# Moving six matmuls of the output layer in front of the fourth product into the C bank

## The chip, the cores and the metric

The kernel runs on one core of a Trainium2 chip. The metric is the device time of one execution in microseconds. The engines have their own instruction queues, each served in order: TensorE (PE, with its weight loads shown as PEld), VectorE (DVE), ScalarE (ACT), GpSimd (POOL) and SyncE (SP), which here only issues DMAs. They wait for one another by semaphores.

## The reference

Two layers in a row, in float32. First an attention over channels, for each of 4 batches of 6080 tokens with 256 channels:

```
qn, kn = q, k divided by their norms over the tokens
a      = softmax(kn^T @ qn / tau)          # 256 x 256 for each batch
x      = v @ a                             # 6080 x 256
h      = max(x @ w_in, 0)                  # 2048 wide
out    = (h * h) @ w_out                   # 256 wide again
```

The kernel multiplies `a` into `w_in` once for each batch, so that the two products left are `v @ (a w_in)` and `h*h @ w_out`.

## The kernel before

**Precision.** A float32 operand is split into a high part and a low part, each rounded to the type that TensorE takes. One product is then three matmuls: high by high, low weights by high, high weights by low. A split takes a cast on ACT (the high part) and a subtraction on DVE (the low part).

**Groups.** After two blocks of tokens that are done in a plain way, the work goes in 184 groups, k = 0 to 183. A group is one block of tokens (512, in the last two blocks of a batch 480) and a quarter of the 2048 hidden channels. Products of both layers are done in the manner of Strassen and Winograd: on halves of the block and halves of the weights, seven block products instead of eight, with sums and differences formed by DVE.

**First layer, three banks of PSUM.** `product` (line 992) issues six matmuls: two parts of the hidden channels by three terms. Group k makes seven such products: `first_B` and `second_B` into a B bank, `first_H` and `second_H` into an H bank, and for the C bank `copy_C` (line 1199: ACT copies B's first product into C), `second_C`, `third_C` and `fourth_C` (line 1217). Between them the C bank is read: `copy_of_C` (ACT, after the second product), `add_C` (DVE, line 1241, after the third product: adds C to a block of x and applies the rectifier), `relu_C` (ACT, line 1235, after the fourth). As the fourth product writes into the bank that `add_C` reads, `fourth_C` waits for `add_C` of the same group. It also issues the loads of the later weight forms of group k + 2.

**Second layer, one group and two groups behind.** The rectified blocks of x are squared on ACT (`square_three`, three of them at once, and `square_last`), and combined on DVE: `two_sums`, `third_sum`, `last_sum`. They are split in three lots: "A" (`hi_A` on ACT, `lo_A` on DVE, lines 1158 and 1163), "S1" (`hi_S`, `lo_S`) and "S2". The products with W_out are windows of six matmuls each: `window_A1`, `window_A2`, `window_A3` use lot A of group k - 1; four `window_S` use lots S1 and S2 of group k - 2. `window_A2` multiplies the block a2 by the weight sum S4 and adds into a part of its own of the output bank. In six groups (`PLAIN`, line 1025) a window has three matmuls and the rest is done without sums.

**The order.** `PERIOD` (line 1279) lists the steps of one period by hand, each with its lag: 0 for the newest group, 1 and 2 for the groups behind. The steps of a period are issued in this order; each engine's queue keeps it. A text in place of a step ("act", "dve", "sq", "pe", "norms", "mid") is a point at which the attention of the next batch, running beside, puts in its own pieces: chunks of q and k with their Gram products, or products of `a` with w_in. At "pe" TensorE gets most of these pieces; "pe" stands between `second_H` and `window_A1`.

In the last period the three A windows are held back and issued later, by a loop of their own.

Of the kernel before, what the change touches and what calls it, by code (L numbers as in the profile page):

```python
# [32 lines left out]
def kernel(  # L33
# [1138 lines left out]
    def lo_S(k, which):  # L1172
        hi, lo = PA[k, which]
        vector.tensor_sub(lo, XG[k][:, :, SLOTS[which], :], hi.bitcast(F32))
# [75 lines left out]
    def next_v(k, j, do, i):  # L1250
        b, n, at_j = groups[k]
        at = order.index((b, n)) + 1
        if at_j == j and at < len(order):
            do(at, i)
# [21 lines left out]
    def lo_S2(k):  # L1276
# [37 lines left out]
        (1, third_sum),  # L1314
        (0, square_three),
        (1, window_A1),
        (1, lambda k: next_v(k, 2, lo_of_v, 1)),
        (1, last_sum),
        (0, fourth_C),
# [1 line left out]
        (None, late_step),  # L1321
        (0, first_sum_of_v),
        (1, lambda k: lo_S(k, "S1")),
        (1, window_A2),
        (0, relu_C),
        (1, lambda k: next_v(k, 1, lo_of_v, 0)),
        (1, window_A3),
# [260 lines left out]
```

## Time and profile before

| | |
|---|---|
| Median of 3 runs | 2068.84 us (2067.64 to 2071.0) |
| The profiled execution's own time | 2066.14 us |
| Its span, first to last instruction | 2064.3 us |
| PE, PEld busy | 2057.3 us, 2014.0 us |
| DVE, ACT busy | 1894.4 us, 1869.1 us |
| POOL busy | 350.6 us |
| Granted TensorE clock | 1.000 |

The profile is of one execution. Matmuls are pipelined: a matmul row lasts 0.28 us, but the next one begins 0.11 us later, so the pace of TensorE is read from starts, not from durations. The whole stretch of the 184 groups lies between about 157 and 2051 us of the span.

### The profile page before, as it was taken

What the parts mean: (1) busy time and instruction counts of PE and PEld (TensorE: products, weight loads), DVE (VectorE), ACT (ScalarE), POOL (GpSimd) and SP (SyncE); (2) the same over time, 40 slices, a digit from 0 to 9 for tenths busy, and PEclk for the clock granted to TensorE, in tenths of its full rate; (3) what the DMA queues carried; (4) which work ended last, traced back from release to release, by engine and by line L of the source; (5) the groups of instructions that cost most, each with busy time, mean ns of one, the idle gap of its engine ahead of it and who ended that gap; (6) DMA issues with size and microseconds to landing.
All of it is one profiled execution on the core that took longest, in us unless ns stands there. A gap on an engine that the chain in (4) does not pass through costs nothing.

```text
span 2064.3 us, 43463 instructions
## 1 busy us (share of the span) xinstructions
PE 2057.3 (100%) x17158; PEld 2014.0 (98%) x17158; DVE 1894.4 (92%) x2195; ACT 1869.1 (91%) x2379; POOL 350.6 (17%) x430
## 2 busy tenths in 40 slices
PE   9999999999999999999999999999999999999999
PEld 8789999999999999999999999999999999999999
DVE  7898999989999999989999999998999888888887
ACT  5888999989999999989989999989988988988987
POOL 0000111211222111211112111211121121121121
PEclk9999999999999999999999999999999999999999
DMA  9777888889999888889999988888999788787785
GB/s 362 226 223 277 262 254 268 244 263 313 306 282 303 287 260 259 246 258 295 292 302 266 335 260 263 252 262 251 294 286 308 235 243 253 236 248 247 237 241 153
DMA packets 258012, 549.78 MB, mean 266 GB/s; under 512 B 26672, under 2 KB 113072, under 8 KB 257808
## 3 DMA queue, kind: packets, MB, share of 16 engines
q1 hardware_dynamic: 201456, 469.02, 66.9%
q0 software_dynamic: 56352, 77.98, 18.8%
q8 instruction: 135, 2.21, 0.4%
q14 instruction: 69, 0.57, 0.1%
HBM read 433.59 MB, written 58.72 MB: 238 GB/s over the span
## 4 chain that ended last, share of the span: by engine, by line
PE 94%; DVE 2%; ACT 2%; DMA 1%; issue 0%; SPq 0%; DVEq 0%; ACTq 0%
PE ps_o L29 42%; PE ps_c L29 18%; PE ps_h L29 13%; PE ps_b L29 11%; PE gram L29 7%; PE ps_w L29 2%; DVE x L29 1%; ACT x L29 1%; DMA acc_w<-wi_kept 0%; DVE s_lo L29 0%; DMA v<-in_vT 0%; DVE A_lo L29 0%; ACT A_hi L29 0%; DMA wf<-wf_kept 0%; PE ps_end L29 0%
## 5 line engine op out<-in xcount | busy, mean ns | idle before, releaser
L29 DVE TENSOR_TENSOR x<-x 128x1024 f32<-128x1024 f32 (+2 forms) x549 | 465.0, 847 | 11.1
L29 PE MATMUL ps_c<-v_hi,wf 128*128 128x256 f32 (+1 forms) x2208 | 473.1, 279 | 1.8 <-DVE x L29 0.9
L29 POOL DMA_DIRECT2D o<-o x225 | 232.7, 1188 | 1344.0 <-ACT o L29 838.2
L29 DVE TENSOR_TENSOR s_lo<-x,s_hi 128x1024 fp32r<-128x1024 f32 (+1 forms) x366 | 441.3, 1207 | 13.5 <-ACT s_hi L29 13.2
L29 ACT CAST s_hi<-x 128x1024 fp32r<-128x1024 f32 (+1 forms) x366 | 382.7, 1046 | 72.8 <-DVE x L29 71.4
L29 ACT ACTIVATE x<-x 128x1536 f32<-128x1536 f32 (+4 forms) x384 | 405.4, 1056 | 34.6 <-DVE x L29 33.2
L29 DVE TENSOR_TENSOR A_lo<-x,A_hi 128x1536 fp32r<-128x1536 f32 (+2 forms) x183 | 313.3, 1712 | 76.3 <-ACT A_hi L29 73.3
L29 PEld LDWEIGHTS ps_c<-v_hi,wf 128*128 128x128 f32 x2208 | 374.0, 188 | 9.1 <-DVE x L29 5.9
L29 PE MATMUL ps_b<-v_hi,wf 128*128 128x256 f32 (+1 forms) x1472 | 309.9, 276 | 0.0
L29 PE MATMUL ps_h<-v_hi,wf 128*128 128x256 f32 (+1 forms) x1472 | 309.9, 276 | 0.0
L29 PE MATMUL ps_c<-v_lo,wf 128*128 128x256 f32 (+1 forms) x1104 | 304.9, 276 | 0.0
L29 ACT CAST A_hi<-x 128x1536 fp32r<-128x1536 f32 (+2 forms) x183 | 264.9, 1448 | 0.0
L29 PEld LDWEIGHTS ps_b<-v_hi,wf 128*128 128x128 f32 x1472 | 249.2, 188 | 0.1
L29 PEld LDWEIGHTS ps_h<-v_hi,wf 128*128 128x128 f32 x1472 | 249.2, 188 | 0.0
L29 PEld LDWEIGHTS ps_c<-v_lo,wf 128*128 128x128 f32 x1104 | 207.6, 188 | 0.1
L29 PE MATMUL ps_b<-v_lo,wf 128*128 128x256 f32 (+1 forms) x736 | 203.1, 276 | 0.0
L29 PE MATMUL ps_h<-v_lo,wf 128*128 128x256 f32 (+1 forms) x736 | 203.1, 276 | 0.0
L29 PE MATMUL ps_o<-A_hi,wo_hi 128*128 128x256 f32 (+1 forms) x897 | 191.2, 277 | 0.0
L29 PE MATMUL ps_o<-A_lo,wo_hi 128*128 128x256 f32 (+1 forms) x897 | 190.0, 276 | 0.0
L29 PE MATMUL ps_o<-A_hi,wo_lo 128*128 128x256 f32 (+1 forms) x897 | 189.9, 276 | 0.0
L29 PE MATMUL ps_o<-s_lo,wS_hi 128*128 128x256 f32 (+1 forms) x549 | 151.6, 276 | 0.3 <-DVE s_lo L29 0.2
L29 PE MATMUL ps_o<-s_hi,wS_hi 128*128 128x256 f32 (+1 forms) x549 | 151.6, 276 | 0.0
(172 smaller groups left out, 5132.2 us busy)
## 6 DMA issues: line engine op xcount, KB each, us to landing
wf<-wf_kept SPq DMA_DIRECT2D x368, 512.0 KB, 5.2
wf<-wf_kept SPq DMA_DIRECT2D x368, 384.0 KB, 5.3
o<-o POOLq DMA_DIRECT2D x114, 256.0 KB, 5.5
qk<-in_k SPq DMA_DIRECT2D x88, 256.0 KB, 5.2
qk<-in_q SPq DMA_DIRECT2D x88, 256.0 KB, 5.4
v<-in_vT SPq DMA_DIRECT2D x76, 256.0 KB, 4.9
out_T<-o POOLq DMA_DIRECT2D x152, 128.0 KB, 4.7
wf_kept<-wS SPq DMA_DIRECT2D x64, 256.0 KB, 5.7
```

Source lines behind the costliest of these rows:

```text
L29: return lambda *args, **kwargs: self.tc.keep_in_program_order(issue(*args, **kwargs))
```

## The change

One entry of the list `PERIOD` moves. `window_A2`, six matmuls for group k - 1, was issued after `fourth_C`, the point "norms" and two DVE steps; it is now issued directly after `window_A1`, ahead of `fourth_C`. No instruction is added or removed, and the steps of the other engines keep their order.

```diff
         (0, square_three),
         (1, window_A1),
+        (1, window_A2),
         (1, lambda k: next_v(k, 2, lo_of_v, 1)),
         (1, last_sum),
         (0, fourth_C),
         (None, "norms"),
         (None, late_step),
         (0, first_sum_of_v),
         (1, lambda k: lo_S(k, "S1")),
-        (1, window_A2),
         (0, relu_C),
         (1, lambda k: next_v(k, 1, lo_of_v, 0)),
         (1, window_A3),
```

So TensorE's order around the change was `third_C`, `second_H`, pieces at "pe", `window_A1`, `fourth_C`, pieces at "norms", `window_A2`, `window_A3`, `first_B` of the next group, and becomes `third_C`, `second_H`, pieces at "pe", `window_A1`, `window_A2`, `fourth_C`, pieces at "norms", `window_A3`, `first_B`.

## Rows read from the trace of the kernel before

**Rows 1.** The page: busy time by engine, and the chain that ended last.

```profile
PE 2057.3 (100%) x17158; PEld 2014.0 (98%) x17158; DVE 1894.4 (92%) x2195; ACT 1869.1 (91%) x2379; POOL 350.6 (17%) x430
...
PE 94%; DVE 2%; ACT 2%; DMA 1%; issue 0%; SPq 0%; DVEq 0%; ACTq 0%
```

**Rows 2.** Waits, whole span, weight loads: us in total, times, longest us.

```profile
PEld ps_c L29 <- DVE x L29: 5.9, 23, 0.4
```

**Rows 3.** Timeline of PE, group 141 (start us, us, instruction), and the next second_C.

```profile
1643.43 0.39 PE L29 MATMUL ps_o<-A_lo,wo_hi 128*128 128x256 f32 x2
1643.69 0.38 PE L29 MATMUL ps_c<-v_hi,wf 128*128 128x256 f32 x1
1643.91 0.28 PE L29 MATMUL ps_c<-v_lo,wf 128*128 128x256 f32 x1
...
1644.36 0.28 PE L29 MATMUL ps_c<-v_hi,wf 128*128 128x256 f32 x1
...
1648.55 0.28 PE L29 MATMUL ps_c<-v_hi,wf 128*128 128x256 f32 x1
```

**Rows 4.** Timeline of ACT, groups 141 to 142; idle time before and its releaser in brackets.

```profile
1644.32 1.49 ACT L29 ACTIVATE x<-x 128x1536 f32<-128x1536 f32 x1 [0.20 <-DVE x L29]
1645.72 0.58 ACT L29 ACTIVATE x<-ps_c 128x512 f32<-128x512 f32 x1
...
1647.66 0.59 ACT L29 COPY ps_c<-ps_b 128x512 f32<-128x512 f32 x1
1648.18 1.48 ACT L29 CAST A_hi<-x 128x1536 fp32r<-128x1536 f32 x1
...
1654.00 1.49 ACT L29 ACTIVATE x<-x 128x1536 f32<-128x1536 f32 x1 [0.20 <-DVE x L29]
```

**Rows 5.** Timeline of DVE, the same stretch.

```profile
1642.95 0.68 DVE L29 CUSTOM_DVE_ANT_0 x<-x,ps_c 128x512 f32<-128x512 f32 x1
...
1649.69 1.76 DVE L29 TENSOR_TENSOR A_lo<-x,A_hi 128x1536 fp32r<-128x1536 f32 x1 [1.20 <-ACT A_hi L29]
...
1652.63 0.68 DVE L29 CUSTOM_DVE_ANT_0 x<-x,ps_c 128x512 f32<-128x512 f32 x1
```

**Rows 6.** All waits of ACT and DVE in 1614.6 to 1973.9 us (groups 139 to 175).

```profile
ACT s_hi L29 <- DVE x L29: 29.9, 29, 1.6
ACT x L29 <- DVE x L29: 7.6, 37, 0.2
...
DVE A_lo L29 <- ACT A_hi L29: 36.7, 37, 1.2
DVE s_lo L29 <- ACT s_hi L29: 2.2, 9, 0.3
```

**Rows 7.** Two stretches: length, busy us and count of PE, PEld, DVE, ACT, POOL; clock, DMA.

```profile
610.00:840.00 230.00, 230.00 (x2031) 230.00 (x2030) 223.62 (x235) 221.64 (x275) 45.42 (x56) 1.00 0.91 275
1614.60:1973.90 359.30, 359.18 (x3111) 355.71 (x3109) 318.21 (x343) 321.66 (x408) 70.93 (x87) 1.00 0.82 244
```

**Rows 8.** Timeline of ACT and DVE, groups 71 to 72.

```profile
921.88 0.60 ACT L29 ACTIVATE x<-ps_c 128x512 f32<-128x512 f32 x1 [0.47 <-PE ps_c L29]
...
926.68 0.59 ACT L29 COPY x<-ps_c 128x512 f32<-128x512 f32 x1 [0.80 <-PE ps_c L29]
...
929.46 0.69 DVE L29 CUSTOM_DVE_ANT_0 x<-x,ps_c 128x512 f32<-128x512 f32 x1 [0.53 <-PE ps_c L29]
```

**Rows 9.** Timeline: fourth_C's last matmul and relu_C of group 43; copy_C, second_C of 70.

```profile
621.22 0.28 PE L29 MATMUL ps_c<-v_hi,wf 128*128 128x256 f32 x1
...
621.53 0.60 ACT L29 ACTIVATE x<-ps_c 128x512 f32<-128x512 f32 x1
...
903.03 0.59 ACT L29 COPY ps_c<-ps_b 128x512 f32<-128x512 f32 x1
...
903.92 0.28 PE L29 MATMUL ps_c<-v_hi,wf 128*128 128x256 f32 x1
```

**Rows 10.** The page's DMA issues: the later weight forms, KB each, us to landing.

```profile
wf<-wf_kept SPq DMA_DIRECT2D x368, 512.0 KB, 5.2
```

## The prediction

> **What bounds the kernel now.** I began with the busy times. TensorE is busy for the whole span and carries 94% of the chain that ended last, with VectorE and ScalarE at 92% and 91% [rows 1]. Read alone, this says that only TensorE's lost time matters. So I looked next for what TensorE waits for: one wait stands out, weight loads into the C bank behind VectorE, 5.9 us in 23 times [rows 2]. The timeline shows whose it is. In group 141 the last window of A ends its starts at 1643.43 + 0.11, and the first matmul of `fourth_C` starts at 1643.69, just behind `add_C`, which ended at 1642.95 + 0.68 = 1643.63 [rows 3, 5]. The reader should see a second loss here: the next matmul starts 0.22 us later (1643.91) and not the usual 0.11, so a wait, however short, costs about 0.11 more. I counted 63 groups whose `fourth_C` begins like this, with a first matmul of 0.38 us as in rows 3; the first starts at 170.53, the last at 1983.60 us, and 37 of them are all the groups from 139 to 175. Together they cost 5.9 + 63 x 0.11 = 12.8 us. That is all that the change aims at.
>
> The last question is who sets the pace where the waits stand, and this is what decides the forecast. In the stretch of those 37 groups, list what ScalarE and VectorE wait for: each other, and nothing else; no row names TensorE [rows 6]. Follow one turn by starts: the square of three blocks at 1644.32, `relu_C` at 1645.72 (1.40), `copy_C` at 1647.66 (1.94, with two more steps of ScalarE in it), `hi_A` at 1648.18 (0.52) [rows 4], `lo_A` at 1649.69 (1.51, it waits for `hi_A`), `add_C` at 1652.63 (2.94, with the two sums) [rows 5], and the next square of three at 1654.00 (1.37) [rows 4]. The sum is 9.68 us, and the 37 groups took 359.30 / 37 = 9.71 each [rows 7]. TensorE alone would need less: in 610 to 840 us it starts 2031 matmuls in 230.00 us without losing any, 0.1132 us each [rows 7], and a group of seven products and seven windows has 84, so 9.51 us. In this stretch the two slower engines turn in a loop of their own, TensorE is 0.20 us a group faster, and its wait in front of `fourth_C` is only the place where it is held back to their pace. Elsewhere, as in 610 to 840 us, it loses nothing and there is nothing to win.
>
> **The change part by part.** No instruction is added or removed; 184 windows of six matmuls (three where the group behind is one of the six plain ones) move ahead of six others. Three things follow.
>
> *The wait for `add_C`.* `fourth_C` now comes 6 x 0.113 = 0.68 us later (0.34 behind plain groups). In group 141 it would come 0.6 us after `add_C`, with no wait. TensorE then runs ahead until something else holds it. Next is `second_C`, which needs `copy_C`: 1648.55 against 1647.66 + 0.59 = 1648.25, a slack of 0.30 us [rows 3, 4]. So TensorE wins the one wait (0.15) and this slack once, and from then on stands in front of `second_C` for the same 0.20 us a group. The gain of the whole stretch is at most 0.15 + 0.30 = 0.45 us, kept at its end when TensorE becomes the slower one again, and not 37 x 0.2 = 7.4 us. If delay from ahead comes into the loop, the gain falls, to 0 or below.
>
> *`relu_C` waits longer.* It needs the end of `fourth_C`, which moves back by 0.68 us. In group 141 that costs nothing: `fourth_C` ends at 1644.36 + 0.28 = 1644.64 and `relu_C` starts at 1645.72, 1.08 later [rows 3, 4]. But in 30 groups, which lie in 16 separate runs between 206.0 and 1549.2 us, `relu_C` starts within 0.15 us of the end of `fourth_C`, as in group 43: 621.22 + 0.28 = 621.50 against 621.53 [rows 9]. They are the groups in which the other batch's pieces make TensorE long. There ScalarE gets the full 0.68, and behind `relu_C` are queued the cast of lot S2, the last square, `copy_C` and `hi_A`. What hides it: in most of these runs ScalarE waits again a little later. After group 71 it stood 0.80 us in front of the copy out of C after `second_C`, a product that does not move, and VectorE stood 0.53 us in front of the next `add_C` [rows 8]. So ScalarE takes up all of the 0.68 and VectorE all but 0.15. Cost about 0 for 13 of the runs, where I take group 71 as typical; 0.38 each if the cover is gone (below).
>
> It is gone in the stretches with Gram products, where ScalarE is busy 221.64 and VectorE 223.62 of 230.00 us [rows 7]. The delay of groups 43 and 44 travels with them until the loop meets TensorE again near group 70, where `second_C` starts at 903.92 and `copy_C` ends at 903.03 + 0.59 = 903.62, a slack of 0.30 [rows 9]. TensorE loses 0.68 - 0.30 = 0.38 us. This happens twice (batches 1 to 2, 2 to 3), and a first time behind a plain group with 0.34 - 0.30 = 0.04: together +0.80.
>
> *Short waits that do vanish.* In the shorter runs (groups 29, 73, 77, 81, 121, 125) one wait of `fourth_C` stands between two stretches that TensorE paces. These go, at up to 0.11 each: 0 to -0.7, I take -0.4, since the delay of 0.15 above eats some.
>
> *What is queued with the moved steps.* `window_A2` needs lot A, as `window_A1` just before it does, and writes into a bank that is open already: no new wait. `fourth_C` issues the loads of the later forms of group k + 2 on SP, so these go out 0.68 us later, in the same order on that queue. They land in 5.2 us [rows 10] and are wanted more than one turn (9.68) after the next `second_C`, 1648.55 + 9.68 = 1658.2, that is 13.6 us after 1644.64: 8.4 us are spare, cost 0. Without this cover TensorE would wait up to 0.68 a group. TensorE's pieces at "norms" still follow `fourth_C` directly, for at most a few groups of each batch; cost 0, between -0.1 and +0.1.
>
> *Sum.* -0.45 + 0.80 - 0.4 = -0.05, with delay carried into the long loop between 0 and 0.45: about +0.2 us. The bounds of these terms alone are -1.2 (all gains, no loss in the Gram stretches) and +6.1 (no cover in any of the 16 runs, 0.38 each). The profiled execution took 2066.14 us, its span 2064.3 and 1.8 around it; with the change 2066.3. The median of the runs shown is 2068.84, 2.7 above it, so I forecast 2069.0 us.
>
> The Trainium skill has a rule that speaks against this. "Perfetto Trace Analysis", section "Identifying Performance Opportunities", says to find the most contended engine, judge TensorE by the busy share of its weight loads, find the gaps on it and make what blocks there start sooner. Weight loads are at 98% here, which agrees that TensorE is nearly full; followed literally the rule promises all 12.8 us. The waits of rows 6 speak against it for the 37 groups.
>
> **The rivals.**
>
> *Faster: TensorE is the bound in the long stretch too.* Then each of the 63 waits is on the path, and the time falls by 12.8 to 2056.0. For it: the busy shares and the chain [rows 1]; that the wait repeats in the same place. Against: a loop that sums to 9.68 of 9.71 us without a wait for TensorE [rows 4 to 7]. It would need that `relu_C`, `add_C` or `copy_C` in that stretch wait for TensorE in a way that the list of waits doesn't show. Half of it, 2062.4, already counts here. Chance 0.11.
>
> *Slower: `relu_C` takes the place of `add_C`.* One mechanism: `fourth_C` 0.68 us later holds ScalarE at `relu_C`, and what it holds comes out at `second_C` after 0.30 of slack. Price 0.38 in each of the 16 runs, 6.1 us in all, 2074.9; it decides where ScalarE has less than 0.68 us of idle time between `relu_C` and its next meeting with TensorE. For it: the two engines have under 9% to spare, and in the Gram stretches under 4% [rows 7]. Against: 0.80 and 0.53 us of waits behind group 71 [rows 8]. Chance 0.14.
>
> *The change doesn't do what it says.* The cover of 0.68 us (0.34 behind plain groups) is too short and `fourth_C` still waits. In the steady stretch the wait is 0.15; at most 0.4 anywhere [rows 2]. The time would be that of before, 2068.8. Chance 0.03.
>
> **How the numbers follow.** The forecast, that the wait moves to `second_C` and the time stays, gets 0.72. A measurement of this kernel can tell about 0.2%, 4.1 us, from no change. The forecast and the case without effect lie inside, 0.75; the faster rival lies outside at -12.8 and at its half, 0.11; the slower one lies outside at +6.1 with most of its weight: 0.14. The range goes from 2064.0, 5 below, for a part of the faster rival and the scatter of the runs (2067.64 to 2071.0), to 2074.5, nearly all of the slower one. It leaves out the faster rival in full and the far ends of the slower.
>
> **What would show it.** In the profile of the changed kernel: no wait of `fourth_C` for `add_C` in groups 139 to 175, but one of `second_C` for `copy_C`, and still 9.7 us a group; more waiting of ScalarE in front of `relu_C`, in the groups with other batches' pieces; `relu_C` in group 141 still without a wait. The forecast is wrong if those 37 groups take 9.5 to 9.6 us each, or if groups 71 to 131 lose a few tenths of a microsecond in each run of four.

## The result, and the profile after

| | before | after |
|---|---|---|
| Median | 2068.24 us (6 runs, 2066.98 to 2071.0) | 2080.76 us (6 runs, 2079.25 to 2082.82) |
| Ratio | | 1.0065 [1.0055, 1.0076] |
| Profiled execution, span | 2066.14, 2064.3 us | 2082.82, 2081.1 us |

The change costs 12.5 us. The forecast was 2069.0 us, its range ended at 2074.5, and "slower" had a chance of 0.14: wrong.

The page after answers to [rows 1]: busy time by engine, and the chain that ended last.

```profile
PE 2062.4 (99%) x17158; PEld 2020.9 (97%) x17158; DVE 1893.8 (91%) x2195; ACT 1870.3 (90%) x2379; POOL 349.8 (17%) x430
...
PE 75%; DVE 12%; ACT 7%; issue 4%; DMA 2%; SPq 1%; DVEq 0%; ACTq 0%
```

The busy times of VectorE and ScalarE are within 1.2 us of before, so no work was added. The chain now runs for a quarter of the span through other engines. That shows where a chain was traced, not a price. The waits say more (who waits, for whom, us in total, times, longest):

```profile
PEld ps_c L29 <- ACT x L29: 9.9, 5, 4.8
ACT qk_parts L29 <- DMA wf_kept<-wS: 9.5, 2, 5.1
...
PEld ps_c L29 <- ACT ps_c L29: 1.2, 4, 0.4
...
PEld ps_c L29 <- DVE x L29: 0.4, 1, 0.4
```

The wait that the change aimed at is gone: 5.9 us in 23 times [rows 2] became 0.4 us, once. Two others have come or grown, few and long: ScalarE waits twice, 9.5 us together, for the stores of wS (before, never), and TensorE for ScalarE behind that, 9.9 us in 5 times (before, 0.7 us in 2). wS is a tile with weight sums of the next batch. A cost that lies in two places can be found by time. I followed the start of `relu_C` through all 184 groups in both traces. The delay of after against before is 0.52 us at group 39, 8.21 at group 40, 8.63 at 44, 10.15 at 45, 10.33 at 87, 16.52 at 88, 16.95 at 175 and 16.76 at 183. Groups 40, 45 and 88 hold 15.4 of 16.8 us. (One profiled execution against another; the medians differ by 12.5.)

What happens at group 40 begins on SP's queue. Its timeline before (start, us, line, transfer):

```profile
562.59 0.33 SPq L462 DMA_DIRECT2D qk<-in_k  x1
562.97 0.42 SPq L463 DMA_DIRECT2D qk<-in_q  x1
563.70 5.51 SPq L978 DMA_DIRECT2D wf<-wf_kept  x4
569.31 4.36 SPq L29 DMA_DIRECT2D wf_kept<-wS  x4
573.76 1.28 SPq L462 DMA_DIRECT2D qk<-in_k  x1
575.09 1.18 SPq L463 DMA_DIRECT2D qk<-in_q  x1
```

And after:

```profile
563.10 0.33 SPq L462 DMA_DIRECT2D qk<-in_k  x1
563.48 0.62 SPq L463 DMA_DIRECT2D qk<-in_q  x1
564.20 1.92 SPq L978 DMA_DIRECT2D wf<-wf_kept  x4
573.13 0.33 SPq L462 DMA_DIRECT2D qk<-in_k  x1
573.51 0.42 SPq L463 DMA_DIRECT2D qk<-in_q  x1
574.03 0.85 SPq L978 DMA_DIRECT2D wf<-wf_kept  x2
574.93 2.86 SPq L29 DMA_DIRECT2D wf_kept<-wS  x4
```

The longest wait of that queue after, in 560 to 590 us:

```profile
SPq L462 <- DVE wS L29: 6.9, 1, 6.9
```

The order is another. Before, the second pair of q and k chunks stood behind the four loads and the four stores of wS; after, it stands ahead of the last two loads and of the stores. It needs the buffer that VectorE reads for its last step on wS, so it stands at the head of the queue for 6.9 us, and nothing behind it leaves between 566.1 and 573.13. Of SP's 1239 transfers 42 stand in another place than before, in ten spots; the two that matter are the ends of the second and of the third batch's weight forms, just ahead of groups 40 and 88. The code shows which could move. The four stores are given to `sync`, the object that keeps the order of the program, and their rows bear its line, 29. The loads of q and k and of the weight forms shown here are given to `nc.sync` (lines 462, 463 and 978) and are not held to that order. In the two traces the 326 transfers of line 29 keep their order among themselves, and the loads of `nc.sync` have moved between them. So whatever places these loads when the program is built placed them anew when TensorE's order changed; by what rule it chooses, no run shows.

ScalarE's timeline after, group 40 (the cast into qk_parts takes over the room that wS held):

```profile
581.37 0.58 ACT L29 COPY ps_c<-ps_b 128x512 f32<-128x512 f32 x1
587.03 1.04 ACT L29 CAST qk_parts<-qk 128x1024 fp32r<-128x1024 f32 x1 [5.08 <-DMA wf_kept<-wS]
...
597.49 0.60 ACT L29 ACTIVATE x<-ps_c 128x512 f32<-128x512 f32 x1 [2.35 <-PE ps_c L29]
```

Before, the last store landed at 578.53 and this cast ran without a wait:

```profile
581.38 1.04 ACT L29 CAST qk_parts<-qk 128x1024 fp32r<-128x1024 f32 x1
```

After, the last store landed at 586.88. ScalarE lost 5.08 us there, and 2.35 more at `relu_C`, which waited for TensorE. Why TensorE was late shows in its own rows. By windows, of TensorE alone (stretch, length, busy us and count, granted clock, DMA share, GB/s):

```profile
586.00:588.00 2.00, 0.00 (x0) 1.00 1.02 402
588.00:590.00 2.00, 0.10 (x1) 0.61 1.06 425
590.00:592.00 2.00, 2.00 (x10) 0.50 1.01 413
592.00:594.00 2.00, 2.00 (x11) 0.50 1.01 385
594.00:596.00 2.00, 2.00 (x14) 0.68 0.44 170
596.00:598.00 2.00, 2.00 (x20) 1.00 0.00 0
```

And its timeline:

```profile
589.90 0.58 PE L29 MATMUL ps_c<-v_hi,wf 128*128 128x256 f32 x1 [4.57 <-ACT x L29]
590.28 0.41 PE L29 MATMUL ps_c<-v_lo,wf 128*128 128x256 f32 x1
590.49 0.63 PE L29 MATMUL ps_c<-v_hi,wf 128*128 128x256 f32 x2
```

TensorE stood idle for 4.57 us, and what it did next ran at half its clock, 0.50 (1.2 of 2.4 GHz): from 589.90 to about 595.2 us its matmuls start 0.213 us apart and not 0.113. These 24 matmuls took 5.3 us; at 0.113 they would take 2.7, which is 2.6 less (an estimate) and covers the 2.35. So 5.08 of waiting and 2.35 behind the slow clock are 7.43 of the 7.69 us that group 40 lost.

### The profile page after: what moved, and what is told of

The parts are those of the page before. It is cut to its first block, busy times and chain, and to the rows that moved or that the text cites. A ratio compares the mean times of both kernels' runs of the same rounds, so it can differ in the third digit from the quotient of the medians.

```text
span 2081.1 us, 43462 instructions
## 1 busy us (share of the span) xinstructions
PE 2062.4 (99%) x17158; PEld 2020.9 (97%) x17158; DVE 1893.8 (91%) x2195; ACT 1870.3 (90%) x2379; POOL 349.8 (17%) x430
## 4 chain that ended last, share of the span: by engine, by line
PE 75%; DVE 12%; ACT 7%; issue 4%; DMA 2%; SPq 1%; DVEq 0%; ACTq 0%
PE ps_o L29 33%; PE ps_c L29 14%; PE ps_h L29 11%; PE ps_b L29 9%; PE gram L29 5%; DVE x L29 4%; ACT x L29 3%; DVE A_lo L29 2%; PE ps_w L29 2%; DVE s_lo L29 2%; ACT A_hi L29 1%; DMA wf_kept<-wS 1%; DVE v_lo L29 1%; DVE qk_parts L29 1%; DMA v<-in_vT 1%
## 5 line engine op out<-in xcount | busy, mean ns | idle before, releaser
L29 PEld LDWEIGHTS ps_c<-v_hi,wf 128*128 128x128 f32 x2208 | 374.9, 188 | 12.8 <-ACT x L29 9.9
```

What stands on the lines that cost most here:

```text
L29: return lambda *args, **kwargs: self.tc.keep_in_program_order(issue(*args, **kwargs))
```

## The experiments

All times are medians from five rounds beside the kernel before, whose median was 2067.29 us in the first four experiments and 2068.02 in the last three.

**SP's order taken back, the window moved.** At the end of the tile function the transfers are tied to one another in the order of before, by places in the program, without a semaphore:

```diff
+    dmas = [i for i in nc.cur_bb.bb.instructions if i.engine == mybir.EngineType.SP and "DMA" in type(i).__name__.upper()]
+    for run in (
+        ...
+        (390, 391, 392, 393, 394, 395, 396, 399, 400, 403),
+        ...
+    ):
+        for one, other in zip(run, run[1:]):
+            tc.add_manual_dep(dmas[other], dmas[one].name, ...)
```

Here 390 is a load of wf_0, 391 and 392 the loads of wf_1 for group 40, 393 to 396 the stores of wS, 399 and 400 the second pair.

> The window moved as in the changed kernel, but SP's queue held in the order that it had before (TensorE's order of the changed kernel, SP's of the kernel before, nothing else differs). Theory (the loss is SP's order: two loads of q and k stand in front of four stores that ScalarE waits for): no wait of 5 us in front of the cast of q and k in groups 40 and 88, time within 2 us of the kernel before, about +1.1 us, 2069.3; groups 139 to 175 still 9.7 us each, with TensorE's wait at second_C. Rival 1 (the move on TensorE itself, relu_C later): the loss stays, about 2080. Rival 2 (only both together cost): about 2069 here and about 2069 with SP's new order alone.

Measured: 2068.2 us, ratio 1.0006 [0.9997, 1.0015]. The cast into qk_parts has no wait, though little was spare: the last store landed at 581.55.

```profile
581.67 1.05 ACT L29 CAST qk_parts<-qk 128x1024 fp32r<-128x1024 f32 x1
```

**The window where it was, SP's order of after.** The same edit on the kernel before, with the order of after, as `(390, 399, 400, 391, 392, 393, 394, 395, 396, 403)`.

> The window where it was before, SP's queue in the order of the changed kernel. Theory: the whole loss comes back without the move, 11 to 15 us, about 2080, with waits of about 5 us in front of the casts of q and k in groups 40 and 88. Rival 1 (the move itself): about 2068. Rival 2 (only both together): about 2069.

Measured: 2078.92 us, ratio 1.0062 [1.0049, 1.0074]; the cast waits 4.49 us:

```profile
586.34 1.04 ACT L29 CAST qk_parts<-qk 128x1024 fp32r<-128x1024 f32 x1 [4.49 <-DMA wf_kept<-wS]
```

That is 11.6 us more than before, so the loss of 12.5 is there, within its scatter, without the change in TensorE's order. The rival that the move itself makes this loss falls: alone, it costs 0.9 us, and 3 at most by the interval of the first experiment.

**Only the second pair put back.** The changed kernel, with only the run above and its like for group 88.

> The changed kernel with one thing of SP's order put back, in two places (end of batch 1's and of batch 2's weight forms): the second pair of loads of q and k stands behind the two weight loads and the four stores of S, no longer in front. Theory: this pair holds the stores, so nearly the whole loss goes, 2069 to 2071. If the first pair or the loads of v matter as much: 2074 or more.

Measured: 2069.89 us, ratio 1.0011 [1.0002, 1.002]. Some 10 of the 12.5 us are gone; 2.6 stay, and the cast still waits 0.77 us at group 40 and 0.78 at group 88.

**Only the first pair put back**, `(386, 387, 388, 397, 398, 389)` and its like:

> The changed kernel with the first pair of loads of q and k put back behind two weight loads, the second pair left in front of the stores. Theory: the loss stays, 2079 to 2082. If the first pair is the cause: 2069 to 2072.

Measured: 2080.51 us, ratio 1.0065 [1.0053, 1.0078]. Putting the first pair back wins nothing that can be seen. In the profiled executions group 45 lost 1.4 to 2.1 us in some kernels and 0.1 or less in others, with SP's order of before among both. The wait behind it is VectorE's, for the next block of v: 2.4 to 3.1 us in the kernels that lost time there, 1.0 at most in the others. Why that load came late in some, no run shows.

**What the pair delays.** As in the third experiment, but with the pair between the loads of wf_1 and the stores: `(390, 391, 392, 399, 400, 393, 394, 395, 396, 403)`.

> The moved window, with the loads of wf_1 for group 40 (and 88) ahead of the second pair of q and k chunks, as in the kernel before, but the pair still ahead of the four stores of wS. It differs from the experiment with the second pair put back only in the places of the pair and the stores. Theory (the stores wait behind a pair that waits for its buffer): ScalarE's cast into qk_parts waits 3.5 to 5 us for the stores in groups 40 and 88 again, and the time is 2077 to 2082 us. Rival (the loads of wf_1 behind the pair were what came late): no such wait over 1 us, and 2069 to 2071 us as with the pair put back.

Measured: 2075.27 us, ratio 1.0034 [1.0021, 1.0047], between the two forecasts. ScalarE, then SP:

```profile
583.93 1.05 ACT L29 CAST qk_parts<-qk 128x1024 fp32r<-128x1024 f32 x1 [2.46 <-DMA wf_kept<-wS]
```

```profile
563.96 5.96 SPq L978 DMA_DIRECT2D wf<-wf_kept  x6
572.64 0.33 SPq L462 DMA_DIRECT2D qk<-in_k  x1
573.03 1.05 SPq L463 DMA_DIRECT2D qk<-in_q  x1
574.12 3.04 SPq L29 DMA_DIRECT2D wf_kept<-wS  x4
```

The stores leave only 0.8 us earlier than after (574.12 against 574.93), yet the last lands at 583.79 and not 586.88. So both explanations were half right. The wait of the queue delays the stores, and it also leaves the transfer engines with less to do: in 566 to 569 us they moved 215 GB/s in after and 316 in this experiment, in 569 to 573 us 327 and 413, in 573 to 577 us 207 and 279. Over these 11 us that is some 0.9 MB, about the two loads of wf_1 (512 KB each), which in after leave only at 574.03 and land ahead of the stores. By medians, each against its own kernel before, the third experiment costs 2.6 us, this one 7.3 and after 12.5: some 5 us for either part.

**Twice the dose of the move.** `window_A3` goes in front of `fourth_C` as well, with SP's order of before.

```diff
         (1, window_A1),
         (1, window_A2),
+        (1, window_A3),
...
         (1, lambda k: next_v(k, 1, lo_of_v, 0)),
-        (1, window_A3),
```

> window_A2 and window_A3 both in front of fourth_C, SP's queue in the order of before. fourth_C is then 1.36 us later than before, twice the dose. Theory (the move costs only where relu_C is held and the hold comes out at second_C): in groups 139 to 175 relu_C starts about 0.1 us behind fourth_C, and the turn stays 9.7 us, since relu_C to second_C (1.94 + 0.59) and the 60 matmuls from second_C to the end of fourth_C (6.8 us) sum to 9.4 to 9.6, under 9.68. In the groups with the other batch's pieces the hold is 1.3 us and not 0.68, more than the waits behind it, so a part stays: 2070 to 2074 us. Rival (the hold is always given back): 2067 to 2069 us. Rival (relu_C is in the loop everywhere): 37 groups at 9.9 us or more, 2076 us or above.

Measured: 2105.28 us, ratio 1.0179 [1.0165, 1.0193]; of what I had written, 2070 to 2074 us is far too low. The time is one that the last rival allows (2076 or above), but not by its cause: the steady groups take less than its 9.9 us. Its groups 139 to 175 (from `relu_C` to `relu_C`), and one turn of ScalarE, then of TensorE there:

```profile
1658.45:2020.36 361.91, 361.91 (x3110) 357.58 (x3109) 318.27 (x343) 323.25 (x408) 67.61 (x83) 1.00 0.80 244
```

```profile
1678.07 0.60 ACT L29 ACTIVATE x<-ps_c 128x512 f32<-128x512 f32 x1
...
1687.86 0.60 ACT L29 ACTIVATE x<-ps_c 128x512 f32<-128x512 f32 x1
```

```profile
1680.68 0.38 PE L29 MATMUL ps_c<-v_hi,wf 128*128 128x256 f32 x1
...
1687.55 0.28 PE L29 MATMUL ps_c<-v_hi,wf 128*128 128x256 f32 x1
```

`relu_C` to `second_C` is 1680.68 - 1678.07 = 2.61 us, from there to the next `relu_C` 7.18: a ring (steps that each wait for the one before, round and round) of 9.79 us, more than the 9.68 of the two slower engines. I had summed this ring to at most 9.6. A safer way is to count its slack: in groups 139 to 175 before, `relu_C` starts 1.07 us behind the end of `fourth_C` and `second_C` 0.29 behind the end of `copy_C` on average; when one waits for the other these are 0.04 and 0.05. So 1.27 us were free. One window takes 0.68, two take 1.36, 0.09 too much, and the turn grew from 9.71 to 361.91 / 37 = 9.78. Outside this stretch it costs more: groups 10 to 24 went from 10.66 to 10.95 us each, 50 to 69 from 10.65 to 10.94, 100 to 111 from 10.84 to 11.09. A mean hides this: in groups 50 to 69 the free slack in the trace before is 1.33 us on average, but about 1.04 in every second group up to 62. What 1.36 exceeds it by, added up group by group over all 184, is 32.9 us, an estimate; the profiled execution grew by 35.3. By stretches the count is rough (3.5 us for a measured 2.5 in groups 139 to 175, 2.9 for 5.1 in 50 to 69), so that the ring makes the whole of this loss is likely and not shown.

**Who paces groups 139 to 175.** The moved window with SP's order of before, and in these groups the square of one block left out:

```diff
     def square_last(k):
-        square(k, a2, a2)
+        if not 139 <= k <= 175:
+            square(k, a2, a2)
```

> The moved window with SP's order of before, and in groups 139 to 175 square_last is left out, so that one of the seven blocks of x goes into the second layer unsquared there: 0.53 us less of ScalarE in each turn of the loop relu_C, copy_C, hi_A, lo_A, add_C. Theory (ScalarE's and VectorE's loop of 9.68 us paces these groups and TensorE alone would need 9.51): the 37 groups take 9.51 to 9.55 us each, 6 to 7.5 us less in all, 2060.5 to 2062.5 us, and no wait of second_C for copy_C is left there. Rival (TensorE paces them): 9.7 us each as with the square, 2067 to 2069 us.

Measured: 2062.48 us, ratio 0.9972 [0.9962, 0.9982]. The 37 groups:

```profile
1630.17:1982.02 351.85, 351.85 (x3105) 351.79 (x3105) 321.05 (x343) 304.47 (x370) 66.97 (x82) 1.00 0.82 250
```

351.85 / 37 = 9.51 us each, what 84 matmuls of 0.1132 us take. With 0.53 us less of ScalarE the pace falls to TensorE's own and no further.

## Why the prediction was wrong, point by point

**The step that failed** is in "What is queued with the moved steps": the loads on SP "go out 0.68 us later, in the same order on that queue", cost 0. The order was not the same. No load of weight forms held TensorE up by more than 0.2 us, and that once, so the cover that I gave them was enough; but what stood beside them on the queue changed places, and the pair of q and k, which is no part of the change, held up four stores that ScalarE needs. The line "the steps of the other engines keep their order", written ahead of the prediction, holds for ScalarE, VectorE and GpSimd, whose instructions stand in the same order in both traces, and not for SP. None of the rivals had this in it. The second experiment shows that it accounts for the loss: 2078.92 us with the window in its old place, against 2067.29.

**The wait for `add_C`: right.** After, groups 139 to 175 have no such wait, and still take 9.71 us each:

```profile
1643.25:2002.45 359.20, 359.20 (x3110) 357.18 (x3110) 317.73 (x343) 320.95 (x407) 66.59 (x81) 1.00 0.81 244
```

TensorE is now held at `second_C`, as forecast. Group 141 after, TensorE and then ScalarE, answers to [rows 3, 4]:

```profile
1661.80 0.28 PE L29 MATMUL ps_c<-v_hi,wf 128*128 128x256 f32 x1
...
1665.36 0.39 PE L29 MATMUL ps_c<-v_hi,wf 128*128 128x256 f32 x1
1665.58 0.28 PE L29 MATMUL ps_c<-v_lo,wf 128*128 128x256 f32 x1
```

```profile
1662.78 0.58 ACT L29 ACTIVATE x<-ps_c 128x512 f32<-128x512 f32 x1
...
1664.72 0.58 ACT L29 COPY ps_c<-ps_b 128x512 f32<-128x512 f32 x1
```

`copy_C` ends at 1665.30, the product starts at 1665.36 with the long first matmul, and the next one is 0.22 us behind. `relu_C` starts 0.70 us behind `fourth_C` (1.08 before) and has no wait. The last experiment shows the reason given, a loop of the slower engines, and with it that the faster rival (12.8 us) was rightly given little. At the end of the stretch 0.25 us were kept; I had said at most 0.45.

**`relu_C` waits longer: right in kind, the Gram term too small.** In the first experiment, which has the move alone, groups 70, 74, 78 and 82 each lose 0.57 to 0.64 us at `relu_C` and gain 0.67 back two groups later, as forecast from [rows 8]; ScalarE's waits at this place rose from 28.3 us in 49 times to 30.4 in 58. In groups 40 to 49 and 88 to 97 it loses 0.99 and 0.91 us, where I had 0.38 each. I had let that loss be set where the loop meets TensorE again near group 70; but it stands by group 49 (1.29 us behind before) and is still the same at group 69 (1.27). And the hold comes out in a place that I left out: the windows of lots S1 and S2 waited for VectorE's `lo_S` for 5.0 us in 16 times, before for 1.0 us in 3. (That it gets there through the cast of lot S2, which is queued behind `relu_C`, follows from the order of the program; no run tests it.) Over all groups the move alone costs 1.4 us in the profiled executions and 0.9 in the medians, within their scatter; I had +0.2. Counted again, the 30 groups lie in 18 runs and not 16, so the slower rival's price was 6.8 us and not 6.1. The slower rival's mechanism is real, and the experiment with two windows shows it in groups 139 to 175; with one window, the ring there has slack left.

**The short waits: about right.** I took -0.4. In the runs of groups 70 to 84 and 118 to 132 the first experiment gains 0.29 each.

## What to carry to other kernels

Before costing a step as moved, ask for every queue who decides its order: one that the program pins stays, one that a planner fills may come out otherwise, and then a transfer that waits for its buffer at the head of the queue holds up everything behind it. When a small edit has a large price, list what changed in each engine's own order first, and follow one step's start through all periods: here a loss in two places was a collision on a queue, and a loss spread over all periods went with a ring that had no slack left. Whether a product may be moved later is read from the slack around its ring, and the next edit of the same size need not be free because the first was.

## What the runs showed of the hardware

A wait of TensorE can cost more than its length: after 4.57 us without work the granted clock was 0.50 for the next 5.3 us, and `relu_C` of group 40 waited 2.35 us for that. In the experiment with the pair ahead of the stores the clock fell after a wait of 2.2 us too: TensorE went on at 586.81 with 1.00, and had 0.52 in 588 to 590 us. The waits of before at the C bank, 0.5 us at most, left it at 1.00. When a weight load had to wait for another engine, its first matmul was 0.22 and not 0.11 us ahead of the next, at `second_C` as at `fourth_C`. And four stores of 256 KB that landed 5 us after their issue before (569.31 to 574.48 for the first) took 9.3 us (574.93 to 584.27) when they were issued right behind the transfers that the same queue had held back. In the four kernels with SP's order of before the first store took 5.2 to 7.0 us, in the three with the pair ahead of the last two loads and the stores 9.3 to 9.8.
